# Two blocks of the first MLP moved into the last attention pair, weight bits through PSUM

## The chip, the core and the metric

The kernel runs on one core of a Trainium2 chip. The metric is device time in microseconds (us) of one execution, lower is better. The engines are PE (TensorE, matrix multiply, with its weight loads as PEld), DVE (VectorE), ACT (ScalarE), POOL (GpSimd) and SP (SyncE, which only issues transfers here). SBUF is the working memory; PSUM is the memory that matmuls write, eight banks of 128 x 512 f32.

## What is computed

Attention over 2 x 8 heads with 1152 keys and 576 pooled queries of width 64 (two neighbouring queries are averaged), then two MLPs over the 1152 resulting tokens, 512 wide inside and 2048 wide in between:

```python
q_pool = q.reshape(B, H, S // 2, 2, D).mean(axis=3)
scores = scale * np.matmul(q_pool, k.transpose(0, 1, 3, 2))
attn = softmax(scores)                      # row maximum subtracted
x = np.matmul(attn, v)                      # tokens: 2 x 576, features: 8 heads x 64
h = x @ w_in;  x = (max(h, 0) + alpha * min(h, 0)) @ w_out
h = x @ w_in2; x = (P(h) / (Q(h) + 1e-6)) @ w_out2
```

## The kernel before, in words

Precision is kept by splitting operands into a high and a low part, so most products are three matmuls. The weights come from memory as 64-bit patterns, and each block of them (128 x 512) is turned into f32 by hand: `w_load` (a transfer issued by SP into a raw slot), `w_abs` (ACT, takes the upper words into a work tile M), `w_shift` and `w_top` (DVE, change M in place, `w_top` with the raw upper words as second input), `w_low` (DVE, ors in the raw lower words), `w_hi` (ACT, high part), `w_lo` (POOL, low part). M is a slot of a small ring in SBUF, `ms`. A table `bits` can instead send the first three steps of a block through a PSUM bank, with `w_low` writing back into an SBUF slot; before, only blocks of the second MLP are in that table.

Everything is placed on one hand-written time axis. A function `at(time, fn, ...)` puts a step at a time in units of one attention step; `NUDGE` shifts single entries; `emit` sorts all entries by time and issues them. So the axis only sets the order on each engine's queue (and in SP's queue of transfers); what really happens when is settled by waits.

Attention runs over 8 pairs of heads (`p` = 0 to 7), 18 steps each: head `o` of the pair, key block `t` of 9. A step is `score` (PE, four matmuls into one of two PSUM buffers `st` of two banks each), `p_exp` (ACT, frees `st`), `p_lo` (DVE for the steps in `TAIL_DVE` or `ON_DVE`, POOL for the others) and, `LAG` = 3.348 steps later, `av` (PE, 15 small matmuls into the bank `o`; two neighbouring steps are put together). After a head, `norm` (DVE) empties bank `o`, and there is only one such bank. After a pair, `x_trans` (PE) turns the result into two banks, `x_hi` (ACT) and `x_lo` (DVE) write it into `xh` and `xl`, the first MLP's input. Inside a pair the row maxima for the next pair are made in the banks `m0`, `m1`, `m2` (`max_mm`, `max_relu`, `max_1`, `max_2`); in the last pair (times 126 to 144) there is no next pair, and these banks hold only the transposed result of pair 6, placed at 141.8.

The first MLP begins at time 144. `mlp_in(u)` is a block of 12 matmuls for step `u` = (layer, third of the tokens, block of the hidden width) into a bank `h0` to `h3`, which take the place of the two `st` buffers. The first four steps are of the first 384 tokens, which come from pairs 0 to 3 alone; from step 4 on the tokens need the last pair. Then come `act` and `prelu` (ACT, DVE), `g_hi` and `g_lo` (ACT, POOL) and `mlp_out` (PE, nine matmuls). The lists `wq` and `w_at` place the weights; the first nine blocks are prepared during pairs 6 and 7.

Of the kernel before, what the change touches and what calls it, by code (L numbers as in the profile page):

```python
# [11 lines left out]
F32 = mybir.dt.float32  # L12
# [9 lines left out]
P = 128  # L22

NUDGE = {
    "act 149.66": -1.83248,
    "act 149.84": 0.05243,
    "act 153.14": 0.05243,
# [5 lines left out]
    "av +15.34": -0.25933,  # L33
# [4 lines left out]
    "av +6.35": 0.11407,  # L38
    "av 118.34": -0.05915,
    "av 121.34": -0.27727,  # L40
    "av 121.35": 0.03902,
    "av 125.34": 0.28986,
    "av 125.35": 0.30551,
# [21 lines left out]
    "g_hi 1": -0.14597,  # L65
    "g_hi 151.56": -0.67127,
    "g_hi 154.86": -0.27922,
# [7 lines left out]
    "g_lo 148.36": 0.18778,  # L75
    "g_lo 154.96": -0.03704,
    "g_lo 244.06": 0.90746,
# [4 lines left out]
    "g_lo 352.74": 0.10763,  # L82
    "init_1 -59.90": -0.34567,
# [9 lines left out]
    "k2_move 108.36": 0.32169,  # L93
# [8 lines left out]
    "last 472.04": 5.6109,  # L102
    "load_k +13.00": 2.48384,
# [13 lines left out]
    "max_1 -51.55": 0.33187,  # L117
    "max_1 113.13": 0.14749,
    "max_1 120.30": -0.07283,
# [7 lines left out]
    "max_2 112.05": 0.42508,  # L127
    "max_2 117.78": 0.15996,
    "max_2 119.21": -0.07283,
# [8 lines left out]
    "max_mm 110.29": -0.29231,  # L138
    "max_mm 112.58": 0.05397,
    "max_mm 114.59": -0.08673,  # L140
    "max_mm 115.44": -0.77992,
    "max_mm 117.46": 0.28459,
    "max_mm 118.89": -0.21705,
    "max_mm 119.74": -0.07283,
    "max_mm 12.24": 0.03862,
    "max_mm 120.32": -0.07283,
    "max_mm 13.39": -0.15071,
    "max_mm 4.88": -0.12388,
    "max_put 13.64": -0.4836,
    "max_put 6.77": -0.05341,  # L150
    "max_relu -50.82": -0.13659,
    "max_relu 108.56": 0.29424,
    "max_relu 11.38": 0.04928,
    "max_relu 112.86": 0.20726,
    "max_relu 120.03": 0.0732,
# [17 lines left out]
    "mlp_consts 128.00": 0.28684,  # L173
    "mlp_in 2": -1.20185,
# [26 lines left out]
    "norm 146.76": 0.03824,  # L201
# [7 lines left out]
    "p_exp +16.45": -0.15163,  # L209
# [4 lines left out]
    "p_exp 121.45": -0.2674,  # L214
    "p_exp 122.45": -0.0253,
    "p_exp 143.45": 0.12204,
# [4 lines left out]
    "p_lo +12.05": 0.04903,  # L221
    "p_lo +2.05": 0.08012,
    "p_lo +5.05": 0.56187,
    "p_lo 1.05": 0.23379,
    "p_lo 11.05": 0.61317,
    "p_lo 113.05": 0.21679,
    "p_lo 122.05": -0.2674,
    "p_lo 123.05": 0.04433,
    "p_lo 124.05": 0.04433,
    "p_lo 128.05": -0.03096,  # L230
    "p_lo 129.05": 0.35293,
    "p_lo 135.05": -0.11243,
    "p_lo 17.05": 0.76834,
    "p_lo 5.05": -0.42349,
    "prelu 1": 0.06312,
    "prelu 160.51": -0.19632,
# [44 lines left out]
    "v_abs 112.00": 0.5906,  # L281
# [22 lines left out]
    "w_hi 125.13": 0.02594,  # L304
# [16 lines left out]
    "w_load 156.72": 0.44095,  # L321
# [35 lines left out]
def attention_then_two_mlps(  # L357
# [14 lines left out]
    nc = tc.nc  # L372
# [19 lines left out]
    psum = ctx.enter_context(tc.tile_pool(name="psum", bufs=1, space=bass.MemoryType.PSUM))  # L392
# [31 lines left out]
    xh = const.tile([P, KT, NTOK], F32R, name="xh")  # L424
    xl = const.tile([P, KT, NTOK], F32R, name="xl")
# [42 lines left out]
    bits = {}  # L468
# [71 lines left out]
    steps = [(0, T, f) for T in range(2) for f in range(NE)] + \  # L540
# [81 lines left out]
    KR, QR, QS, QH, QL, KH, KL, VR, VS, AM, X, NM, O, ST, TS = ({} for _ in range(15))  # L622
# [363 lines left out]
    for p in range(NP):  # L986
        b = S2 * p
        if p >= 2:
            k = S2 * (p - 2) + (-5.0 if p > 2 else 1.5)
            at(k, load_q, p)  # L990
            at(k, load_k, p)
            prep_at(S2 * (p - 2) + (5.2 if p > 2 else 9.6), p)
        if p >= 1:
            if p > 1:
                at(b - 23.0, load_v, p)
            m0, md = (b - 11.505, 1.15) if p == 1 else (b - 17.721, 1.433)
            for j in range(NJ2):
# [55 lines left out]
    for i in range(4):  # L1053
        at(k + (0.2, 1.285, 4.529, 5.1)[i], mlp_in, steps[i])
# [128 lines left out]
    for s, u in enumerate(steps):  # L1183
        L, T, f = u
# [90 lines left out]
```

## Time and profile before

| | before |
|---|---|
| time, median of 3 runs | 659.12 us (658.53 to 660.01) |
| the profiled execution | span 657.9 us from first to last instruction |
| busy share of the span | PE 96%, PEld 87%, DVE 76%, ACT 74%, POOL 63% |
| granted PE clock, mean over the span | 0.986 of full |

The profile is of one execution; the time of a run also holds what lies around the span. On this kernel the last attention pair lies at about 210 to 248 us of the span. Busy shares are means over stages with different limits.

### The profile page before, as it was taken

What the parts mean: (1) busy time and instruction counts of PE and PEld (TensorE: products, weight loads), DVE (VectorE), ACT (ScalarE), POOL (GpSimd) and SP (SyncE); (2) the same over time, 40 slices, a digit from 0 to 9 for tenths busy, and PEclk for the clock granted to TensorE, in tenths of its full rate; (3) what the DMA queues carried; (4) which work ended last, traced back from release to release, by engine and by line L of the source; (5) the groups of instructions that cost most, each with busy time, mean ns of one, the idle gap of its engine ahead of it and who ended that gap; (6) DMA issues with size and microseconds to landing.
All of it is one profiled execution on the core that took longest, in us unless ns stands there. A gap on an engine that the chain in (4) does not pass through costs nothing. (4 is left out here: it accounts for less than half of the span.)

```text
span 657.9 us, 13614 instructions
## 1 busy us (share of the span) xinstructions
PE 632.2 (96%) x5186; PEld 573.7 (87%) x5186; DVE 501.7 (76%) x941; ACT 485.6 (74%) x902; POOL 412.8 (63%) x350
## 2 busy tenths in 40 slices
PE   7789999999999789999999999999999999999997
PEld 6679999999998689999999999999898889999995
DVE  7877786876969988998851169996889777777764
ACT  6668778787887566677653478888888888778774
POOL 6557687787857775786762227785466745444443
PEclk7989999999999899999999999999999999999999
DMA  4887968869751225443420006641320010001001
GB/s 179 219 206 172 226 146 215 177 161 235 148 160 66 99 79 179 146 143 128 161 97 0 1 33 222 223 134 62 128 81 16 1 48 1 1 0 49 1 0 48
DMA packets 20960, 72.28 MB, mean 110 GB/s; under 512 B 3104, under 2 KB 3104, under 8 KB 20896
## 3 DMA queue, kind: packets, MB, share of 16 engines
q1 hardware_dynamic: 20896, 71.42, 37.6%
q8 instruction: 40, 0.66, 0.4%
q14 instruction: 24, 0.20, 0.1%
HBM read 47.72 MB, written 2.36 MB: 76 GB/s over the span
## 5 line engine op out<-in xcount | busy, mean ns | idle before, releaser
L874 POOL TENSOR_TENSOR PL<-PF 128x576 f16<-128x576 f32 x106 | 140.6, 1343 | 55.3 <-ACT PF L868 52.2
L1128 POOL TENSOR_TENSOR gl<-g,gh 128x384 fp32r<-128x384 f32 x96 | 106.4, 1108 | 74.5 <-ACT gh L1124 56.1
L868 ACT ACTIVATE PF<-st 128x576 f32<-128x576 f32 x144 | 91.7, 650 | 36.1 <-PE st L860 34.9
L1139 PE MATMUL acc<-woh,gl 128*128 128x512 f32 x288 | 113.8, 395 | 0.8 <-POOL gl L1128 0.8
L1139 PE MATMUL acc<-woh,gh 128*128 128x512 f32 x288 | 113.1, 393 | 0.7 <-ACT m L1170 0.7
L1139 PE MATMUL acc<-wol,gh 128*128 128x512 f32 x288 | 113.1, 393 | 0.0
L860 PE MATMUL st<-QQ,K 128*128 128x288 f32 (+1 forms) x576 | 103.9, 307 | 1.3 <-ACT PF L868 1.3
L1098 POOL TENSOR_TENSOR b<-a,b 128x384 f32<-128x384 f32 x48 | 49.0, 1020 | 78.1 <-ACT b L1086 78.1
L860 PEld LDWEIGHTS st<-QQ,K 128*128 128x128 f32 (+1 forms) x576 | 88.1, 193 | 2.7 <-ACT PF L868 1.7
L529 PE MATMUL hp<-xh,wih 128*128 128x384 f32 x384 | 83.4, 339 | 0.0
L529 PE MATMUL hp<-xl,wih 128*128 128x384 f32 x384 | 83.1, 338 | 0.0
L529 PE MATMUL hp<-xh,wil 128*128 128x384 f32 x384 | 83.0, 338 | 0.0
L886 PE MATMUL o<-V,PF 128*128 128x65 f16 x720 | 78.2, 196 | 2.9 <-DVE x L901 2.9
L773 PE MATMUL m<-K,QQ 128*128 128x384 f32 x234 | 72.0, 375 | 8.3 <-issue 2.5
L890 PE MATMUL o<-V,PL 128*128 128x65 f16 x720 | 76.6, 193 | 2.3 <-POOL PL L874 1.8
L886 PEld LDWEIGHTS <-PF 128*128 128x128 bf16 x720 | 67.0, 98 | 12.2 <-DVE x L901 3.3
L888 PE MATMUL o<-V,PF 128*128 128x64 f16 x720 | 77.3, 197 | 0.0
L529 PEld LDWEIGHTS hp<-xh,wih 128*128 128x128 f32 x384 | 69.6, 188 | 7.6
L890 PEld LDWEIGHTS <-PL 128*128 128x128 f16 x720 | 67.9, 100 | 2.7 <-POOL PL L874 2.0
L1124 ACT ACTIVATE gh<-g 128x384 fp32r<-128x384 f32 x96 | 50.0, 521 | 26.1 <-DVE g L1089 17.5
L529 PEld LDWEIGHTS hp<-xh,wil 128*128 128x128 f32 x384 | 68.7, 188 | 0.0
L529 PEld LDWEIGHTS hp<-xl,wih 128*128 128x128 f32 x384 | 68.6, 188 | 0.0
(143 smaller groups left out, 1360.5 us busy)
## 6 DMA issues: line engine op xcount, KB each, us to landing
K<-kh SPq DMA_DIRECT2D x28, 384.0 KB, 5.6
ring<-in_w SPq DMA_DIRECT2D x19, 512.0 KB, 3.6
raw<-in_w SPq DMA_DIRECT2D x13, 512.0 KB, 3.5
ring<-in_w1o SPq DMA_DIRECT2D x10, 512.0 KB, 3.4
qr<-in_qT SPq DMA_DIRECT2D x8, 576.0 KB, 7.6
vr<-in_v SPq DMA_DIRECT2D x8, 576.0 KB, 7.6
ring<-in_w2o SPq DMA_DIRECT2D x9, 512.0 KB, 4.3
QQ<-qh SPq DMA_DIRECT2D x14, 288.0 KB, 3.9
```

The costliest lines, as they stand in the source:

```text
L529: nc.tensor.matmul(hp, lhsT=w_[:, c * P:(c + 1) * P], rhs=x_[:, c, ts], start=k == 0, stop=k == 3 * KT - 1)
L773: nc.tensor.matmul(s[:, 0:CW], lhsT=of(QQ, n)[:, 0, k * P:(k + 1) * P], rhs=of(K1, n)[:, k0:k0 + CW], start=n == parts[0][0], stop=n == pa ...
L860: nc.tensor.matmul(st[:, hf, 0:HALF], lhsT=k_[:, ks], rhs=q_[:, c:c + HALF], start=first, stop=not first)
L868: nc.scalar.activation(out=PF[buf(n, t)][:, 0:SQ].rearrange("p (h q) -> p h q", h=2), in_=ST.pop((n, t))[:, :, 0:HALF], func=AF.Exp, scale=SC)
L874: e.tensor_tensor(out=PL[u][:, 0:SQ], in0=PF[u][:, 0:SQ], in1=top(PF[u])[:, 0:SQ], op=ALU.subtract)
L886: nc.tensor.matmul(o, lhsT=ph, rhs=V16[i][:, t, 0:D + 1], start=first, stop=False, skip_group_check=True)
L888: nc.tensor.matmul(o[:, 1:D + 1], lhsT=ph, rhs=V16[i][:, t, D + 1:2 * D + 1], start=False, stop=False, skip_group_check=True)
L890: nc.tensor.matmul(o, lhsT=pl, rhs=V16[i][:, t, 0:D + 1], start=False, stop=last, skip_group_check=True)
L1098: nc.gpsimd.tensor_tensor(out=E[u, "b"], in0=E[u, "a"], in1=E[u, "b"], op=ALU.mult)
L1124: nc.scalar.activation(out=G[u][0], in_=E[u, "g"], func=AF.Copy)
L1128: nc.gpsimd.tensor_tensor(out=gl, in0=E[u, "g"], in1=gh.bitcast(F32), op=ALU.subtract)
L1139: nc.tensor.matmul(acc, lhsT=g_[:, cs], rhs=w_, start=f == 0 and k == 0, stop=f == NF - 1 and k == 2)
```

## The change

Four things are changed. (1) Of the nine weight blocks that are prepared in pairs 6 and 7, the last six (`i >= 3`) send their bits through the bank `m0`. (2) `mlp_in` of the first two MLP steps (`EARLY = 2`) is cut into three parts of four matmuls, placed at 131.5, 133.5, 135.5 and 137.5, 139.5, 141.5 inside the last pair, into the banks `m1` and `m2`. (3) The transposes of pair 6 go from 141.8 to 130.2; those of pair 7 use `h0` and `h1` instead of `m1` and `m2`. (4) Some 200 entries of `NUDGE`, nearly all at times 108 to 161, are new or other. No instruction is added or taken out.

```diff
 NUDGE = {
...
+    "mlp_in 131.50": -0.04134,
+    "mlp_in 135.50": -0.97833,
+    "mlp_in 139.50": 0.50456,
+    "mlp_in 141.50": 0.73288,
+    "mlp_in 148.53": 0.41771,
...
-    "norm 146.76": 0.03824,
+    "norm 128.76": -0.05062,
+    "norm 146.76": 0.13528,
...
+    "p_lo 144.05": 0.08084,
...
+    "w_low 142.74": 1.10529,
...
+    EARLY = 2
...
     def hp_tag(u):
         s = steps.index(u)
+        if s < EARLY:
+            return f"m{s + 1}"
         return f"h{s % (2 if 4 <= s < PASS_B + 4 else 3 if PASS_B <= s < PASS_B + NF else 4)}"
 
-    def mlp_in(u):
+    def mlp_in(u, parts=(0, 1, 2)):
         L, T, f = u
         ts = slice(T * TOK, (T + 1) * TOK)
-        hp = HP[u] = bank(hp_tag(u), "hp")[:, 0:TOK]
+        if 0 in parts:
+            HP[u] = bank(hp_tag(u), "hp")[:, 0:TOK]
         wh, wl = W[L, f, "i"]
-        k = 0
-        for w_, x_ in ((wh, xh), (wh, xl), (wl, xh)):
+        for i in parts:
+            w_, x_ = ((wh, xh), (wh, xl), (wl, xh))[i]
             for c in range(KT):
-                nc.tensor.matmul(hp, lhsT=w_[:, c * P:(c + 1) * P], rhs=x_[:, c, ts],
-                                 start=k == 0, stop=k == 3 * KT - 1)
-                k += 1
+                nc.tensor.matmul(HP[u], lhsT=w_[:, c * P:(c + 1) * P], rhs=x_[:, c, ts],
+                                 start=i == c == 0, stop=i == 2 and c == KT - 1)
...
-            tp = X[p, c] = psum.tile([P, 512], F32, tag=f"m{c}", name="xtp")
+            tp = X[p, c] = bank(f"m{c}" if p + 1 < NP else f"h{c - 1}", "xtp")
...
-        x_at(b + S2 + 15.786 if p + 1 < NP else b + S2 + 5.0, p)
+        x_at(b + S2 + (15.786 if p + 2 < NP else 4.2 if p + 1 < NP else 5.0), p)
...
     for i, w in enumerate(wq[:NW]):
+        if i >= 3:
+            bits[w] = "m0"
         w_at(k + 0.475 + 3.778 * i, (4.178, 4.635, 5.665, 6.817, 8.104, 8.937), *w)
     k = S2 * NP
     at(k + 0.1, hp_rooms)
-    for i in range(4):
+    for i in range(EARLY):
+        for j in range(3):
+            at(k - 12.5 + 6 * i + 2 * j, mlp_in, steps[i], (j,))
+    for i in range(EARLY, 4):
         at(k + (0.2, 1.285, 4.529, 5.1)[i], mlp_in, steps[i])
```

## Rows read from the trace of the kernel before

**Rows 1.** Windows: us, busy by engine (instructions), granted clock, transfers.
```profile
210.00:220.00 10.00, 8.12 (x134) 7.31 (x130) 9.93 (x11) 6.81 (x13) 8.76 (x7) 1.00 0.18 56
220.00:230.00 10.00, 7.46 (x112) 7.24 (x113) 9.89 (x15) 5.95 (x11) 6.36 (x6) 0.83 0.29 107
230.00:240.00 10.00, 7.93 (x135) 7.07 (x134) 7.78 (x13) 6.06 (x11) 7.50 (x5) 1.00 0.20 68
...
260.00:280.00 20.00, 20.00 (x103) 18.26 (x102) 19.72 (x21) 12.48 (x25) 14.82 (x12) 1.00 0.38 139
```

**Rows 2.** Waits of PE, 200 to 246 us: us in total, times, longest.
```profile
PE o L886 <- DVE x L901: 2.9, 1, 2.9
PE o L890 <- POOL PL L874: 1.8, 2, 1.3
```

**Rows 3.** Timeline of DVE, 216 to 220 us: start, us, instruction.
```profile
216.09 0.78 DVE L478 TENSOR_SCALAR ring<-ring 128x512 int32<-128x512 int32 x1
216.91 1.52 DVE L483 SCALAR_TENSOR_TENSOR ring<-ring 128x512 int32<-128x512 int32 x1
218.46 1.52 DVE L491 SCALAR_TENSOR_TENSOR ring<-ring 128x512 int32<-128x512 int32 x1
```

**Rows 4.** Windows around PE's longest wait, columns as in Rows 1.
```profile
220.00:222.00 2.00, 0.00 (x0) 0.00 (x0) 1.93 (x4) 1.99 (x4) 2.00 (x2) 1.00 0.44 154
223.00:227.00 4.00, 4.00 (x57) 3.85 (x54) 3.96 (x6) 2.14 (x4) 1.06 (x2) 0.57 0.04 8
```

**Rows 5.** Line of POOL, 222 to 236 us: count, ns minimum/median/maximum, first and last start.
```profile
L874 POOL TENSOR_TENSOR PL<-PF x4: 1143/1462/4167, 222.7 to 235.7; 128x576 f16<-128x576 f32 x4
```

**Rows 6.** Groups of DVE, 208 to 245 us: count, busy us, mean ns, idle before.
```profile
L491 DVE SCALAR_TENSOR_TENSOR ring<-ring 128x512 int32<-128x512 int32 x4 | 4.5, 1126 | 0.0
L483 DVE SCALAR_TENSOR_TENSOR ring<-ring 128x512 int32<-128x512 int32 x4 | 4.2, 1053 | 0.0
L483 DVE SCALAR_TENSOR_TENSOR m<-ring,m 128x512 int32<-128x512 int32 x2 | 3.3, 1642 | 0.0
L478 DVE TENSOR_SCALAR ring<-ring 128x512 int32<-128x512 int32 x4 | 2.5, 632 | 0.0
...
L491 DVE SCALAR_TENSOR_TENSOR m<-ring,m 128x512 int32<-128x512 int32 x2 | 1.6, 789 | 0.0
...
L478 DVE TENSOR_SCALAR m<-m 128x512 int32<-128x512 int32 x2 | 1.0, 514 | 0.0
```

**Rows 7.** Lines of DVE, 400 to 560 us, columns as in Rows 5.
```profile
L483 DVE SCALAR_TENSOR_TENSOR bits<-ring,bits x14: 685/695/697, 402.1 to 512.4; 128x512 int32<-128x512 int32 x14
...
L478 DVE TENSOR_SCALAR bits<-bits x26: 687/692/700, 401.4 to 511.3; 128x512 int32<-128x512 int32 x26
...
L491 DVE SCALAR_TENSOR_TENSOR ring<-ring,bits x10: 677/686/689, 405.1 to 513.5; 128x512 int32<-128x512 int32 x10
```

**Rows 8.** Single line of DVE, 208 to 245 us, columns as in Rows 5.
```profile
L478 DVE TENSOR_SCALAR ring<-ring x4: 411/600/916, 208.3 to 232.0; 128x512 int32<-128x512 int32 x4
```

**Rows 9.** Timeline of PE, 238 to 268 us.
```profile
238.84 0.74 PE L917 MATMUL xtp<-ident,x 128*128 128x128 f32 x5
239.77 1.33 PE L860 MATMUL st<-QQ,K 128*128 128x288 f32 x8 [0.19 <-ACT PF L868]
...
242.00 0.97 PE L529 MATMUL hp<-xh,wih 128*128 128x384 f32 x4
...
246.33 0.20 PE L886 MATMUL o<-V,PF 128*128 128x65 f16 x1
...
267.11 0.39 PE L1139 MATMUL acc<-woh,gh 128*128 128x512 f32 x1
```

**Rows 10.** Timeline of DVE, 243 to 246 us.
```profile
243.17 0.81 DVE L925 TENSOR_TENSOR xl<-xtp,xh 128x512 fp32r<-128x512 f32 x2
...
244.72 0.75 DVE L874 TENSOR_TENSOR PL<-PF 128x576 f16<-128x576 f32 x1
```

**Rows 11.** Timeline of POOL, 264 to 266 us.
```profile
264.47 1.47 POOL L1128 TENSOR_TENSOR gl<-g,gh 128x384 fp32r<-128x384 f32 x1
```

More of the change, by code (lines that the diff above doesn't have):

```diff
@@ L24 @@
 NUDGE = {
-    "act 149.66": -1.83248,
+    "act 146.36": -1.10603,
+    "act 149.66": -1.72223,
     "act 149.84": 0.05243,
-    "act 153.14": 0.05243,
+    "act 152.96": 0.28197,
+    "act 153.14": 0.14335,
+    "act 156.26": -5.29814,
+    "act 156.44": -1.39004,
     "act 255.26": -0.04173,
@@ L32 @@
     "av +11.35": -0.00272,
-    "av +15.34": -0.25933,
+    "av +15.34": -0.05229,
+    "av +15.35": 0.10315,
     "av +17.35": 0.2086,
@@ L38 @@
     "av +6.35": 0.11407,
+    "av 109.34": 0.1927,
+    "av 109.35": 0.35589,
+    "av 114.35": 0.04355,
+    "av 116.34": -0.30193,
     "av 118.34": -0.05915,
[L40 to L43, printed above, removed]
+    "av 118.35": 0.48044,
+    "av 119.35": -0.29911,
+    "av 121.34": -0.94225,
+    "av 121.35": 0.06912,
+    "av 123.35": 0.12304,
+    "av 125.34": -0.02717,
+    "av 125.35": 0.44388,
+    "av 127.34": -0.28253,
     "av 130.34": 0.12379,
     "av 130.35": 0.38061,
+    "av 134.34": -0.21855,
+    "av 134.35": -0.05604,
+    "av 136.34": -0.02503,
+    "av 139.34": -0.50419,
+    "av 141.34": -0.0173,
     "av 143.34": -0.13888,
+    "av 143.35": 0.37695,
+    "av 145.34": -0.02526,
+    "av 145.35": 0.26536,
+    "av 146.35": 0.05461,
     "av 4.34": -0.09646,
@@ L65 @@
     "g_hi 1": -0.14597,
+    "g_hi 148.26": -0.05578,
     "g_hi 151.56": -0.67127,
-    "g_hi 154.86": -0.27922,
+    "g_hi 154.86": -0.34847,
+    "g_hi 158.16": -0.0454,
     "g_hi 2": 0.09897,
@@ L74 @@
     "g_hi 461.30": 0.10728,
-    "g_lo 148.36": 0.18778,
+    "g_lo 151.66": 0.29516,
     "g_lo 154.96": -0.03704,
+    "g_lo 158.26": 0.84439,
     "g_lo 244.06": 0.90746,
@@ L82 @@
     "g_lo 352.74": 0.10763,
+    "hp_rooms 144.10": 0.09744,
     "init_1 -59.90": -0.34567,
@@ L92 @@
     "k2_move +11.50": 4.60114,
-    "k2_move 108.36": 0.32169,
+    "k2_move 108.36": -0.36613,
     "k_diff +6.50": 0.25928,
@@ L102 @@
     "last 472.04": 5.6109,
+    "last_pair_rooms 126.50": 0.80603,
     "load_k +13.00": 2.48384,
@@ L117 @@
     "max_1 -51.55": 0.33187,
+    "max_1 108.83": -0.23804,
+    "max_1 111.70": 0.06062,
     "max_1 113.13": 0.14749,
-    "max_1 120.30": -0.07283,
+    "max_1 114.56": -0.03607,
+    "max_1 116.00": -0.13946,
+    "max_1 118.86": 0.04418,
     "max_1 15.10": -0.21038,
@@ L126 @@
     "max_2 -52.20": -0.12622,
-    "max_2 112.05": 0.42508,
+    "max_2 109.18": -0.22946,
+    "max_2 110.61": 0.04636,
+    "max_2 112.05": 0.95768,
+    "max_2 113.48": 0.3681,
     "max_2 117.78": 0.15996,
-    "max_2 119.21": -0.07283,
+    "max_2 119.21": 0.18431,
+    "max_2 120.64": -0.0839,
     "max_2 13.14": -0.24061,
@@ L137 @@
     "max_mm 0.58": -0.05411,
[L138 to L143, printed above, removed]
+    "max_mm 108.28": 0.25225,
+    "max_mm 108.86": 0.05718,
+    "max_mm 110.29": -0.24239,
+    "max_mm 112.58": 0.1727,
+    "max_mm 113.16": -0.27666,
+    "max_mm 114.01": -0.07202,
+    "max_mm 114.59": -0.13974,
+    "max_mm 116.88": -0.45352,
+    "max_mm 117.46": 0.15243,
+    "max_mm 118.89": -0.15077,
     "max_mm 119.74": -0.07283,
     "max_mm 12.24": 0.03862,
-    "max_mm 120.32": -0.07283,
+    "max_mm 120.32": -0.49667,
     "max_mm 13.39": -0.15071,
     "max_mm 4.88": -0.12388,
+    "max_put 122.58": 0.27584,
     "max_put 13.64": -0.4836,
@@ L151 @@
     "max_relu -50.82": -0.13659,
-    "max_relu 108.56": 0.29424,
     "max_relu 11.38": 0.04928,
-    "max_relu 112.86": 0.20726,
-    "max_relu 120.03": 0.0732,
+    "max_relu 110.00": -0.23787,
+    "max_relu 112.86": 0.24883,
+    "max_relu 120.03": -0.10014,
     "max_relu 7.93": 0.56196,
     "max_rows +14.31": -0.08493,
+    "max_rows 122.31": 0.05726,
     "max_rows 13.37": -0.4561,
@@ L160 @@
     "max_split 12.24": 0.27587,
+    "max_split 121.18": -0.04134,
     "max_split 16.84": 0.72017,
@@ L173 @@
     "mlp_consts 128.00": 0.28684,
+    "mlp_consts 133.00": 0.16871,
+    "mlp_in 131.50": -0.04134,
[3 more added lines that the diff above has]
+    "mlp_in 148.53": 0.41771,
+    "mlp_in 158.20": -0.0609,
     "mlp_in 2": -1.20185,
@@ L182 @@
     "mlp_out 1": -2.76993,
+    "mlp_out 153.25": 0.1283,
+    "mlp_out 156.55": 0.04691,
     "mlp_out 3": -0.14864,
@@ L186 @@
     "mlp_out 466.75": 0.51976,
+    "mlp_rooms 150.50": -0.42802,
     "newton 307.86": 0.15744,
@@ L208 @@
     "p_exp +10.45": -0.06749,
-    "p_exp +16.45": -0.15163,
+    "p_exp +15.45": 0.18536,
+    "p_exp +16.45": -0.11413,
+    "p_exp +17.45": -0.06943,
     "p_exp +6.45": -0.11489,
@@ L213 @@
     "p_exp 117.45": 0.3022,
-    "p_exp 121.45": -0.2674,
+    "p_exp 119.45": 0.02991,
+    "p_exp 120.45": -0.11183,
+    "p_exp 121.45": -0.36953,
     "p_exp 122.45": -0.0253,
-    "p_exp 143.45": 0.12204,
+    "p_exp 124.45": 0.30542,
+    "p_exp 125.45": -0.05638,
+    "p_exp 126.45": -0.38716,
+    "p_exp 127.45": -0.47427,
+    "p_exp 128.45": 0.26012,
+    "p_exp 130.45": 0.03501,
+    "p_exp 132.45": -0.16805,
+    "p_exp 136.45": -0.09432,
+    "p_exp 140.45": -0.07307,
+    "p_exp 141.45": -0.07144,
+    "p_exp 142.45": 0.09075,
+    "p_exp 143.45": 0.24749,
     "p_exp 3.45": 0.46905,
@@ L221 @@
     "p_lo +12.05": 0.04903,
+    "p_lo +16.05": 0.15039,
+    "p_lo +17.05": 0.10815,
     "p_lo +2.05": 0.08012,
@@ L224 @@
     "p_lo 1.05": 0.23379,
+    "p_lo 108.05": 1.71774,
+    "p_lo 109.05": 0.96994,
     "p_lo 11.05": 0.61317,
-    "p_lo 113.05": 0.21679,
-    "p_lo 122.05": -0.2674,
-    "p_lo 123.05": 0.04433,
+    "p_lo 110.05": -0.26813,
+    "p_lo 111.05": 1.75388,
+    "p_lo 112.05": -0.91528,
+    "p_lo 113.05": -0.47992,
+    "p_lo 114.05": 1.43444,
+    "p_lo 116.05": 0.0379,
+    "p_lo 118.05": 0.46394,
+    "p_lo 119.05": -0.24861,
+    "p_lo 120.05": 0.30854,
+    "p_lo 121.05": -0.06126,
+    "p_lo 123.05": 0.18759,
     "p_lo 124.05": 0.04433,
-    "p_lo 128.05": -0.03096,
+    "p_lo 125.05": 0.4012,
+    "p_lo 127.05": 0.13444,
+    "p_lo 128.05": 0.23929,
     "p_lo 129.05": 0.35293,
+    "p_lo 130.05": 1.0792,
+    "p_lo 132.05": 0.51744,
+    "p_lo 133.05": 0.35944,
     "p_lo 135.05": -0.11243,
+    "p_lo 137.05": -0.14399,
+    "p_lo 138.05": 0.49851,
+    "p_lo 139.05": 2.20425,
+    "p_lo 141.05": 0.9817,
+    "p_lo 142.05": -0.22956,
+    "p_lo 144.05": 0.08084,
     "p_lo 17.05": 0.76834,
@@ L235 @@
     "prelu 1": 0.06312,
-    "prelu 160.51": -0.19632,
+    "prelu 150.61": -0.66085,
+    "prelu 153.91": -0.32945,
+    "prelu 157.21": 0.76971,
+    "prelu 160.51": -0.48479,
     "prelu 252.91": -0.76034,
@@ L267 @@
     "score 0.00": 0.035,
+    "score 108.00": -0.04102,
     "score 110.00": 0.1155,
+    "score 111.00": -0.41693,
     "score 112.00": -0.46662,
-    "score 113.00": -0.60286,
-    "score 118.00": 0.37261,
-    "score 120.00": 0.1067,
+    "score 113.00": -0.73168,
+    "score 116.00": -2.6424,
+    "score 119.00": -0.18599,
+    "score 120.00": -1.45253,
     "score 121.00": -0.41706,
     "score 122.00": -0.93559,
+    "score 123.00": 0.13775,
+    "score 124.00": 0.27913,
     "score 125.00": -0.7719,
-    "score 135.00": -0.55352,
-    "score 141.00": 0.06003,
+    "score 127.00": -2.66496,
+    "score 128.00": 0.02083,
+    "score 129.00": -0.06616,
+    "score 132.00": -0.07978,
+    "score 134.00": -0.0657,
+    "score 135.00": -0.55352,
+    "score 136.00": -0.293,
+    "score 137.00": -0.58351,
+    "score 138.00": 0.00442,
+    "score 139.00": -0.29725,
+    "score 142.00": 0.20166,
     "score 8.00": -0.42927,
@@ L280 @@
     "v_abs -49.53": 2.0347,
-    "v_abs 112.00": 0.5906,
+    "v_abs 112.00": 0.63011,
     "v_hi +14.96": -2.44725,
@@ L284 @@
     "v_hi 1.97": -0.0338,
-    "v_hi 122.96": -0.05458,
+    "v_hi 113.19": 0.20356,
+    "v_hi 131.19": 0.20924,
     "v_hi 14.96": 0.46325,
+    "v_lo +15.69": -1.30354,
     "v_lo +5.92": 0.08909,
-    "v_lo 123.69": -0.0255,
+    "v_lo 113.92": 0.17612,
+    "v_lo 131.92": -0.28225,
     "v_max +5.40": 0.37337,
     "v_max -47.98": 1.78699,
+    "v_max 113.40": 0.2898,
     "v_max 9.38": 0.15233,
@@ L295 @@
     "w_abs 1": 0.08196,
+    "w_abs 121.21": -0.29279,
+    "w_abs 124.99": -0.35527,
+    "w_abs 128.76": 0.12472,
     "w_abs 132.54": -0.19784,
-    "w_abs 153.93": 0.30825,
+    "w_abs 136.32": 0.2053,
+    "w_abs 140.10": 0.44434,
+    "w_abs 153.93": 0.37728,
     "w_abs 157.06": 0.44095,
-    "w_abs 160.20": 0.47734,
+    "w_abs 160.20": 0.41807,
     "w_abs 2": -0.46434,
@@ L303 @@
     "w_hi 0": 0.24713,
-    "w_hi 125.13": 0.02594,
+    "w_hi 132.69": -0.06541,
+    "w_hi 136.47": 0.16651,
+    "w_hi 140.25": -0.02612,
+    "w_hi 144.02": 0.12937,
+    "w_hi 147.80": 0.25057,
     "w_hi 154.45": 0.15249,
@@ L310 @@
     "w_lo 0": 0.256,
-    "w_lo 118.41": -0.47373,
-    "w_lo 133.52": 0.51392,
+    "w_lo 118.41": -0.60898,
+    "w_lo 133.52": 0.20586,
+    "w_lo 137.30": -0.02673,
+    "w_lo 141.08": 4.02398,
     "w_lo 144.86": -0.31586,
-    "w_lo 148.64": 0.21196,
-    "w_lo 154.55": 2.59363,
+    "w_lo 148.64": 2.50932,
+    "w_lo 154.55": 2.39976,
     "w_lo 157.69": 0.44095,
+    "w_lo 160.82": 1.41328,
     "w_lo 2": 3.88308,
@@ L320 @@
     "w_load 117.03": 0.09064,
-    "w_load 156.72": 0.44095,
+    "w_load 120.81": -0.38484,
+    "w_load 128.37": -0.05019,
+    "w_load 135.92": 0.26143,
+    "w_load 147.31": -1.89704,
+    "w_load 150.44": -3.78195,
+    "w_load 153.58": 0.47245,
+    "w_load 156.72": 0.61107,
     "w_load 159.85": 0.44095,
@@ L324 @@
     "w_load 296.83": -0.17914,
-    "w_low 116.29": 0.08664,
+    "w_low 116.29": 0.18019,
+    "w_low 120.07": -0.0845,
     "w_low 123.85": -0.53747,
-    "w_low 135.18": -0.07142,
-    "w_low 146.52": -0.14543,
+    "w_low 135.18": -0.68451,
+    "w_low 138.96": -0.20937,
+    "w_low 142.74": 1.10529,
+    "w_low 146.52": -0.08582,
+    "w_low 153.17": -0.57349,
+    "w_low 156.30": 0.20595,
+    "w_low 159.44": 0.25883,
     "w_low 352.60": 0.14453,
@@ L331 @@
     "w_shift 121.67": -0.2674,
-    "w_shift 125.44": 0.73028,
+    "w_shift 125.44": 0.83144,
+    "w_shift 136.78": 0.08967,
+    "w_shift 140.56": 0.0275,
     "w_shift 151.44": -0.25643,
+    "w_shift 154.58": -0.02618,
+    "w_shift 157.71": 0.20611,
+    "w_shift 160.85": 0.24925,
     "w_shift 300.53": 0.17955,
@@ L336 @@
     "w_top 0": 0.51732,
-    "w_top 115.14": 0.76013,
+    "w_top 115.14": 0.02872,
     "w_top 118.92": -0.77142,
-    "w_top 130.25": -0.2934,
+    "w_top 130.25": 0.26819,
+    "w_top 134.03": -0.40551,
     "w_top 141.59": 0.95071,
-    "w_top 152.53": 0.36648,
     "w_top 155.67": 0.44095,
@@ L346 @@
     "warm -58.62": 1.87459,
-    "x_hi +16.29": -0.36444,
-    "x_hi 124.29": -0.41997,
-    "x_hi 142.29": -0.2355,
+    "x_hi +16.29": 0.24347,
+    "x_hi 124.29": 0.06389,
     "x_hi 149.50": 0.35742,
+    "x_lo +16.69": 0.91515,
     "x_trans +15.79": -0.03344,
-    "x_trans 123.79": -0.36729,
+    "x_trans 123.79": -0.32324,
 }
```

## The prediction

> **What bounds the kernel now.** I read the page's busy shares first, then windows of ten us, then the waits of PE, then single timelines where PE stood still. PE is busy for 96% of the span, so time can be won only where PE is idle or slow. In the first MLP it is neither: 260:280 is full, at full clock [rows 1]. It is idle inside the last pair: 1.88 us in 210:220, 2.54 in 220:230 and 2.07 in 230:240, together 6.5 us, and in the same windows DVE is busy for 9.93, 9.89 and 7.78 of 10 [rows 1]. So the last pair is paced by DVE, not by PE.
>
> The waits say how. The longest is 2.9 us: the first `av` of the pair's first head waits for `norm` of the head before, which frees the one bank `o` [rows 2]. DVE had no idle time ahead of that `norm`; it was late, with `w_shift`, `w_top` and `w_low` of one weight block (0.78, 1.52, 1.52 us) close in front of it [rows 3]. That wait costs a second time: PE does nothing from 220 to 222 us, and in 223:227 the granted clock is 0.57 on average, that is mostly the lower of its two levels (1.2 instead of 2.4 GHz) [rows 4]. Over 4 us that loses 4 x 0.43 = 1.7 us. The next wait, 1.3 us, is for a `p_lo` on POOL [rows 2]; the longest of these instructions took 4.17 us where the shortest took 1.14 [rows 5].
>
> **Weight bits through PSUM.** In 208:245 DVE did the three bit steps of six blocks out of SBUF: 4.2 + 3.3 us of L483, 4.5 + 1.6 of L491, 2.5 + 1.0 of L478, together 17.1 us or 2.85 per block [rows 6]. The second MLP shows the same steps with the bits in PSUM: 0.695, 0.692 and 0.686 us in the median, 2.07 per block, and within 0.02 us of that every time [rows 7]. Six blocks change over, so DVE gets 6 x 0.78 = 4.7 us shorter. `w_shift` alone gets longer (0.69 against 0.58 on average); the two steps with two inputs get shorter, since out of SBUF their means lie between 0.79 and 1.64 us [rows 6].
>
> POOL is busy for 6.4 to 8.8 of 10 us where they are slow [rows 1]. The Trainium skill, SBUF — State Buffer, section Who interferes with whom, states it as a rule: a VectorE instruction with two SBUF inputs contends with a GpSimd instruction that reads SBUF, one with at most one such input does not. By that rule the trace agrees: bits in PSUM leave one SBUF input, and the spread is gone. The Trainium skill, VectorE: DVE Perf Modes, section Why PSUM operands drop a tier, speaks against the change: a PSUM operand holds f32 work at the plain rate. The trace agrees: the fastest `w_shift` out of SBUF took 0.41 us [rows 8], out of PSUM all took 0.69. By that page alone, with nothing won on the other two, six blocks would make DVE 6 x 0.28 = 1.7 us longer; by the rows it is 4.7 us shorter, and the rows decide.
>
> What is this worth on PE? The fourth block is the one in front of the late `norm`: 3.82 us there [rows 3] become 2.07, so `norm` comes 1.75 us earlier and the wait of 2.9 shrinks to 1.15. Bounds: nothing (if DVE is then held elsewhere) to 2.9. I take 1.75. The 2.07 us of idle time in 230:240 left the clock at 1.00 [rows 1], so I take it that the 1.7 us of slow clock go too; if not, they stay in the sum.
>
> `m0` is one bank for six blocks, where a ring gave slack: `w_abs` of the next block waits on ACT until `w_low` of the last is done, with `p_exp` queued behind it. By the times given these two stand 0.04 steps apart once (143.84 and 143.88) and 0.9 steps or more otherwise; the price is at most one `w_low`, 0.69 us [rows 7], once. I take 0.
>
> **Two blocks moved.** In the old order the 24 matmuls run from 242.00 to 246.33 us, 4.33 us [rows 9]. They leave that place: -4.33. They cost the same in the last pair, +4.33, less what they fill of idle PE time. Behind the first piece lie the 2.07 us of idle time in 230:240 [rows 1]. Bounds of the fill: 0 to 2.07, plus whatever new slack the pieces find. I take 2.07: the idle time is in pieces of up to 1.3 us, and a piece is 4.33/6 = 0.72 us, so it fits in without holding the scores long. The blocks need weights finished long before and tokens of pairs 0 to 3, so nothing else can hold them but their banks.
>
> **What the move uncovers.** In the old order these blocks also hid the end of the pair: the last scores end at 239.77 + 1.33 = 241.10, the last `p_lo` on DVE at 244.72 + 0.75 = 245.47 [rows 9, 10], 4.4 us later, and PE spent 4.33 of them on the two blocks. Now only `av` work stands there. One pair of steps of it fills 241.10 to 242.00, 0.9 us [rows 9]; two such pairs stand between the last score and the last `av`, 1.8 us. If DVE is as late as before, PE idles 4.4 - 1.8 = 2.6 us; if DVE is free, it doesn't. DVE is 4.7 us lighter by then and xl of pair 6 (0.81 us [rows 10]) no longer stands there. I take 0.7.
>
> **Transposes of pair 6.** Work is the same. But the first piece needs the bank `m1`, so it waits on PE until `x_lo` of pair 6 has read it, with all later scores behind it. In the old place the chain from transposes to the end of xl took 238.84 to 243.98, 5.1 us [rows 9, 10], of which the transposes and xl themselves are 1.55; the rest is ACT's part and queueing. PE has 0.74 us of transposes, 0.9 of `av` and half of 1.33 of scores [rows 9] in between: 2.3 us. So the stall is 0 to 2.8. In the new place only two 0.69 us steps [rows 7] are placed between `norm` and xl on DVE, so I take 0.4. The transposes of pair 7 use free banks of the same kind: 0.
>
> **The rest of the order.** The other shifts (pair 6, first MLP steps) move instructions of equal cost. I count nothing; the 1.88 us of idle time in 210:220 [rows 1] bound a gain, and a loss could be as large. The front of the MLP must follow: in 260:280 DVE is busy for 19.72 of 20 [rows 1], and PE uses a `gl` at 267.11 that is ready at 264.47 + 1.47 = 265.94 [rows 9, 11], 1.2 us of slack. PE can get more than 1.2 us ahead only if DVE does too; its 4.7 us allow that.
>
> **Sum.** -4.33 + 4.33 - 2.07 - 1.75 - 1.7 + 0.7 + 0.4 = -4.4 us. The profiled span is 657.9; the median of the runs is 659.12, 1.2 more, which I leave as it is. Span 653.5, time 654.7 us.
>
> **Rivals.** (a) A new wait takes the place of the old one: the chain of pair 6 stays at 5.1 us, the first piece stands 2.8 us at the head of PE's queue, and as after the old wait the clock falls, 1.7. With scores held that long the fill of 2.07 is lost. -1.75 - 1.7 + 0.7 + 2.8 + 1.7 = +1.8, 660.9 us, slower. It decides from a chain of some 4.6 us on. For it: DVE is full there. Against: the bit steps in front of xl are among those that get shorter. Chance 0.08.
>
> (b) The contention only moves: POOL then meets the ten `p_lo` on DVE that still read SBUF twice, `norm` is as late as before, and the clock falls. -2.07 + 0.7 + 0.4 = -1.0, 658.1, no difference to be measured. The MLP front gives the same limit, 1.2. Chance 0.1.
>
> (c) The tail stays open: 2.6 instead of 0.7, so -2.5, 656.6 us. Chance 0.15.
>
> (d) All waits of PE in the pair go, since POOL too is freed: 6.5 + 1.7 - 0.7 - 0.4 = 7.1, 652.0 us. By the Trainium skill's rule on contention (SBUF — State Buffer, section Who interferes with whom), only the weight steps stop contending, not the `p_lo` on DVE, which speaks for a part of it. Chance 0.12.
>
> The forecast, between the others, has 0.55. About 0.2%, 1.3 us, is what a measurement here can tell from no change. Faster: 0.55 + 0.15 + 0.12 = 0.82; same 0.1; slower 0.08. The range reaches from (d) to (b) and its bounds: 651.8 to 658.4.
>
> **What would show it.** L483 and L491 on bits at 0.69 us in the last pair. PE's wait for `norm` near 1.2 us and the clock at 1.00 throughout 220:230. Pieces of `mlp_in` between scores, with less than 4.5 us of idle PE from 210 us to the end of the scores. After the last score an idle PE of under 1 us. If instead the longest wait is that of a piece for xl, (a) holds; if it is still for `norm`, (b). The prediction is wrong at its root if the pair gets longer by the whole 4.3 us, that is if PE was not truly free there.

## The result

The changed kernel took 652.78 us in the median of 5 runs (651.85 to 656.65), the old one beside it 660.01 (658.53 to 661.81): a ratio of 0.990 with a 95% interval of 0.9873 to 0.9926, so 4.9 to 8.4 us faster. 4.4 us were forecast. The profiled spans are 650.8 and 657.9 us.

Not all of these 7.1 us of span come from the last pair: the first twelve heads, hardly touched by the change, took from 189.4 to 195.3 us in the traces of this study. A cleaner measure is the rest of the span behind the `norm` of head 11 (heads counted from 0; it starts at 190.56 us in the old trace and 189.81 in the new). It is 467.34 us before and 460.99 after, 6.35 us less. All comparisons of traces below use it, and call it the rest.

Windows of the new kernel, columns as in [rows 1]:

```profile
210.00:220.00 10.00, 8.00 (x124) 7.18 (x122) 9.86 (x15) 7.81 (x15) 8.89 (x7) 1.00 0.34 106
220.00:230.00 10.00, 10.00 (x163) 9.76 (x161) 9.87 (x17) 6.94 (x14) 5.09 (x6) 1.00 0.17 57
230.00:240.00 10.00, 10.00 (x179) 9.71 (x178) 8.33 (x14) 7.08 (x13) 5.62 (x5) 1.00 0.39 121
240.00:250.00 10.00, 9.87 (x65) 8.80 (x62) 8.61 (x16) 7.61 (x17) 6.30 (x6) 1.00 0.57 207
...
260.00:280.00 20.00, 20.00 (x103) 18.05 (x102) 19.76 (x22) 13.40 (x26) 16.12 (x12) 1.00 0.41 144
```

PE has no idle time left from 220 to 240 us, where it had 4.6 [rows 1], and the granted clock is at its upper level throughout. What is left is 2.0 us in 210:220. The waits of PE from 200 to 246 us:

```profile
PE st L1003 <- ACT PF L1011: 0.9, 1, 0.9
PE xtp L1060 <- DVE x L1044: 0.9, 1, 0.9
PE o L1029 <- DVE x L1044: 0.4, 1, 0.4
PE o L1033 <- POOL PL L1017: 0.2, 1, 0.2
```

The wait of 2.9 us for `norm` [rows 2] is gone. (The second line is the transposes' wait for a `norm`; the transposes of pair 6 now stand ahead of the `av` that waited before. The third line is of another `norm`, at 205 us.) The timeline of DVE ahead of that `norm`, to be laid beside [rows 3]:

```profile
215.24 0.68 DVE L619 TENSOR_SCALAR bits<-bits 128x512 int32<-128x512 int32 x1
215.96 0.70 DVE L624 SCALAR_TENSOR_TENSOR bits<-ring,bits 128x512 int32<-128x512 int32 x1
216.69 0.69 DVE L632 SCALAR_TENSOR_TENSOR m<-ring,bits 128x512 int32<-128x512 int32 x1
217.29 1.26 DVE L1017 TENSOR_TENSOR PL<-PF 128x576 f16<-128x576 f32 x1
218.48 0.15 DVE L1042 TENSOR_SCALAR sm<-o 128x5 f32<-128x5 f32 x1
```

3.82 us of bit steps became 2.07, and `norm` (the last line) starts 3.05 us earlier than before, 2.3 of it won behind the `norm` of head 11. All six blocks run at that rate (lines by tile, 205 to 250 us: count, ns minimum/median/maximum):

```profile
L619 DVE TENSOR_SCALAR bits<-bits x6: 684/692/700, 215.2 to 239.6; 128x512 int32<-128x512 int32 x6
L624 DVE SCALAR_TENSOR_TENSOR bits<-ring,bits x6: 680/693/697, 216.0 to 240.3; 128x512 int32<-128x512 int32 x6
L632 DVE SCALAR_TENSOR_TENSOR ring<-ring,bits x4: 673/681/689, 222.4 to 241.1; 128x512 int32<-128x512 int32 x4
L632 DVE SCALAR_TENSOR_TENSOR m<-ring,bits x2: 679/683/687, 216.7 to 232.9; 128x512 int32<-128x512 int32 x2
```

GpSimd gains as well. Its `p_lo` took up to 4.17 us [rows 5]; now, from 218 to 245 us, the longest takes 1.66:

```profile
L1017 POOL TENSOR_TENSOR PL<-PF x7: 1143/1147/1659, 217.9 to 237.7; 128x576 f16<-128x576 f32 x7
```

And the pieces of the first two MLP blocks stand between the scores, each four matmuls (timeline of PE, 222 to 243 us; the last line is already the third block, behind the last scores). From the start of a piece to the start of the next instruction it is 0.71 to 0.79 us; the column shows more, since the next instruction starts before the piece has ended:

```profile
221.63 0.91 PE L673 MATMUL hp<-xh,wih 128*128 128x384 f32 x4
224.47 0.87 PE L673 MATMUL hp<-xl,wih 128*128 128x384 f32 x4
227.26 0.87 PE L673 MATMUL hp<-xh,wil 128*128 128x384 f32 x4
230.55 0.95 PE L673 MATMUL hp<-xh,wih 128*128 128x384 f32 x4
...
240.29 0.94 PE L673 MATMUL hp<-xh,wih 128*128 128x384 f32 x4
```

### The profile page after: what moved, and what is told of

It reads as the page before. It is cut to its first block, busy times and chain, and to the rows that moved or that the text cites. A ratio compares the mean times of both kernels' runs of the same rounds, so it can differ in the third digit from the quotient of the medians.

```text
span 650.8 us, 13635 instructions
## 1 busy us (share of the span) xinstructions
PE 630.1 (97%) x5186; PEld 571.3 (88%) x5186; DVE 496.2 (76%) x941; ACT 485.8 (75%) x902; POOL 408.0 (63%) x350
## 5 line engine op out<-in xcount | busy, mean ns | idle before, releaser
L1017 POOL TENSOR_TENSOR PL<-PF 128x576 f16<-128x576 f32 x106 | 136.8, 1304 | 56.3 <-ACT PF L1011 52.8
L1029 PE MATMUL o<-V,PF 128*128 128x65 f16 x720 | 76.7, 194 | 0.4 <-DVE x L1044 0.4
L1031 PE MATMUL o<-V,PF 128*128 128x64 f16 x720 | 75.9, 196 | 0.0
```

Source lines behind the costliest of these rows:

```text
L1017: e.tensor_tensor(out=PL[u][:, 0:SQ], in0=PF[u][:, 0:SQ], in1=top(PF[u])[:, 0:SQ], op=ALU.subtract)
L1029: nc.tensor.matmul(o, lhsT=ph, rhs=V16[i][:, t, 0:D + 1], start=first, stop=False, skip_group_check=True)
L1031: nc.tensor.matmul(o[:, 1:D + 1], lhsT=ph, rhs=V16[i][:, t, D + 1:2 * D + 1], start=False, stop=False, skip_group_check=True)
```

## Experiments: which part makes the gain

The theory is that of the prediction: VectorE paced the last pair through bit steps that met GpSimd at SBUF; bits in PSUM take that away, and the blocks then fill idle PE time. The rivals: the moved blocks do it alone, the new order does it, or the ring slots that the bits set free do it. Under each run stands what was expected of it.

Here the change has three parts: the bits, the move (the blocks with the transposes) and the new order, which is the table `NUDGE`. That makes eight combinations, the old and the new kernel among them. Here are the other six.

**Bits alone** (`e1_bits`), in the old kernel:

```diff
     for i, w in enumerate(wq[:NW]):
+        if i >= 3:
+            bits[w] = "m0"
```

> The old kernel with one change alone: the last six weight blocks send their bits through the bank m0. Theory (VectorE paced the last pair because its two-input bit steps out of SBUF met GpSimd): the norm in front of PE's longest wait comes about 1.75 us earlier, the wait falls from 2.9 to about 1.2, the clock stays at full, and the kernel is 2 to 4 us faster. Rival (the moved blocks alone make the gain): within 1 us of the old kernel.

**The move with the new order, without the bits** (`e2_move`): the new kernel without these two lines.

> The new kernel without the bits in PSUM (they stay in the SBUF ring), all else as in the new kernel. Theory: the pieces only fill the idle time behind the long wait, so about 2 us faster than the old kernel, with a wait for norm of over 2 us and bit steps of up to 1.5 us and more. Rival (the moved blocks alone): 5 to 7 us faster, like the new kernel.

**Bits and move with the old order** (`e3_oldorder`): the new kernel with the old `NUDGE`.

> The new kernel with the old table of shifts. Theory (the structure makes the gain, the shifts only polish it): 4 to 6 us faster than the old kernel. Rival (the new order is what makes it): under 2 us faster, or slower.

**The new order alone** (`e4_neworder`): the old kernel with the new `NUDGE`.

> The old kernel with the new table of shifts; entries of steps that it lacks do nothing. Theory (structure): within 1.5 us of the old kernel, to either side. Rival (order): 2 us faster or more.

**The move alone** (`e7_move_old`): the new kernel without the bits and with the old `NUDGE`.

> The moved blocks without the bits in PSUM and with the old table of shifts: the corner that is missing. Theory as the first four runs leave it (without lighter VectorE work the pair stays as long, the pieces only lengthen it and the end loses its cover): within 2 us of the old kernel, PE idle by 2 us or more behind the last scores. Rival (it was the new order that spoilt the move when run without the bits): 2 us faster or more.

**Bits with the new order, no move** (`e8_bits_new`): the new kernel with the blocks and the transposes in their old places and banks.

> The bits in PSUM with the new table of shifts, but no moved blocks. Theory (the new order is made for the moved blocks): about as fast as the bits with the old order, 2.5 to 4 us faster than the old kernel. Rival (the new order wins 1 us by itself once VectorE is lighter): 4 to 5 us faster.

| bits | move | new order | kernel | ratio to the old kernel (95%) | rest of the span, us against old |
|---|---|---|---|---|---|
| | | | old | 1 | 0 |
| | | x | e4_neworder | 1.0011 (0.9992 to 1.0031) | +0.55 |
| | x | | e7_move_old | 0.9992 (0.9980 to 1.0004) | -0.13 |
| | x | x | e2_move | 1.0022 (1.0003 to 1.0041) | +0.89 |
| x | | | e1_bits | 0.9956 (0.9936 to 0.9976) | -3.41 |
| x | | x | e8_bits_new | 0.9971 (0.9955 to 0.9987) | -3.23 |
| x | x | | e3_oldorder | 0.9914 (0.9887 to 0.9940) | -5.13 |
| x | x | x | new | 0.9900 (0.9873 to 0.9926) | -6.35 |

The last column is one execution each, the ratio is the timing; they agree within a us but for `e8_bits_new` (0.9971 is 1.9 us, the trace says 3.2). Kernels that gain nothing lie between -0.18 and +0.89 in that column (two of them follow below), so one us there is not told from chance. Three things follow. The bits are the root: with them every combination is faster, without them none measurably is. The move is worth nothing without them; with them it is worth 1.7 to 3.1 us by the traces (-5.13 against -3.41, -6.35 against -3.23) and 2.8 to 4.7 by the timings, and in the new order the two intervals lie well apart. The new order is worth 1.2 us by the traces where both other parts are there and costs 0.2 to 1.0 elsewhere; this is not shown, since it is no more than the scatter and the intervals of the last two lines overlap.

`e1_bits` came out by the theory in its details too: `norm` came 2.18 us earlier behind that of head 11, 0.9 us of PE's wait for it were left, and the clock was at full. `e3_oldorder`, `e4_neworder` and `e7_move_old` lie where the theory put them; `e8_bits_new` does by the trace, while its timing is under the 2.5 us.

The expectation of 2 us for `e2_move` failed, and with it a step of the prediction (the fill, below). The pieces did fill idle time, but the idle time came back behind them. In the move alone, PE in 244:247 us, then its waits from 238 to 252 us, then DVE there:

```profile
244.00:247.00 3.00, 1.73 (x32) 1.61 (x33) 2.97 (x4) 1.63 (x3) 1.71 (x2) 1.00 0.16 44
```

```profile
PE o L892 <- POOL PL L876: 0.9, 1, 0.9
PE xtp L919 <- DVE x L903: 0.9, 1, 0.9
PE o L892 <- DVE PL L876: 0.6, 1, 0.6
```

```profile
241.86 1.77 DVE L483 SCALAR_TENSOR_TENSOR m<-ring,m 128x512 int32<-128x512 int32 x1
243.66 1.52 DVE L491 SCALAR_TENSOR_TENSOR m<-ring,m 128x512 int32<-128x512 int32 x1
245.11 0.75 DVE L876 TENSOR_TENSOR PL<-PF 128x576 f16<-128x576 f32 x1
```

This is the end of the pair: the last `p_lo` waits on DVE behind two bit steps of 1.77 and 1.52 us, and the `av` on PE for it. In the old order the two blocks stood here as cover [rows 9, 10]. DVE is busy for 2.97 of the 3 us in which PE is for 1.73. So without a lighter DVE the blocks only change places with idle time.

**The place of the operand or the ring** (`e6_slack`): the new kernel with the six blocks' bits in one SBUF slot of their own.

```diff
+    extra.append(hold.tile([P, DM], F32, name="extra"))
...
-        M[L, f, nm] = bank(tag, "bits") if tag else take(ms)
+        M[L, f, nm] = extra[0] if tag == "sbuf" else bank(tag, "bits") if tag else take(ms)
...
-            bits[w] = "m0"
+            bits[w] = "sbuf"
```

> The new kernel, but the six blocks' bits go through one slot of SBUF of their own instead of the bank m0. The ring gets the same relief and the blocks the same single slot, but the two-input steps read SBUF twice. Theory (it is the place of the operand: two SBUF inputs meet GpSimd): slow bit steps of 1.4 us and more are back, the wait for norm is over 2 us, time within 2 us of the old kernel. Rival (the ring slots are what helps): 5 to 7 us faster, like the new kernel.

1.0013 (0.9996 to 1.0029), rest +0.05 us: nothing is left of the gain, though the ring has the same relief. The bit steps, 205 to 250 us:

```profile
L620 DVE TENSOR_SCALAR extra<-extra x6: 427/696/1219, 218.7 to 248.9; 128x512 int32<-128x512 int32 x6
L625 DVE SCALAR_TENSOR_TENSOR extra<-ring,extra x6: 691/1518/1775, 219.6 to 249.3; 128x512 int32<-128x512 int32 x6
L633 DVE SCALAR_TENSOR_TENSOR ring<-ring,extra x3: 679/682/691, 228.5 to 247.4; 128x512 int32<-128x512 int32 x3
L633 DVE SCALAR_TENSOR_TENSOR m<-ring,extra x2: 680/1100/1519, 221.1 to 241.7; 128x512 int32<-128x512 int32 x2
```

For `w_top` (the second line): same instruction, same shape, same place in the order, and 0.69 us in the median with one operand in PSUM, 1.52 with both in SBUF. It is the place of the operand.

Not every step with two SBUF inputs is slow, as the third line shows. What tells the slow ones from the others is GpSimd. In the old kernel (lines of POOL and DVE): from 216.54 to 220.99 us GpSimd is at work on `p_lo`, and both two-input bit steps that fall into it take 1.52 us [rows 3]; from 237.30 to 239.79 it has nothing to do, and `w_low`, one of the two, takes 0.68:

```profile
216.54 4.45 POOL L874 TENSOR_TENSOR PL<-PF 128x576 f16<-128x576 f32 x3
239.79 1.15 POOL L874 TENSOR_TENSOR PL<-PF 128x576 f16<-128x576 f32 x1 [2.50 <-ACT PF L868]
237.84 0.68 DVE L491 SCALAR_TENSOR_TENSOR ring<-ring 128x512 int32<-128x512 int32 x1
```

So it is in all fourteen traces of this study, from 196 to 250 us. The 41 two-input bit steps out of SBUF beside which no GpSimd instruction ran took 0.68 or 0.69 us each; the 130 that met one took 0.68 to 1.77; the 88 with an operand in PSUM took 0.67 to 0.70, GpSimd or not. The Trainium skill, SBUF — State Buffer, section Who interferes with whom, has the rule: a VectorE instruction with two SBUF inputs contends with a GpSimd instruction that reads SBUF, and one with a single SBUF input does so only in the modes that use two ports. The traces agree on the two-input steps. The prediction gave the rule without its second condition, and that is too short: `w_shift` out of SBUF, with one input, took 0.41 to 0.43 us beside an idle GpSimd (25 times) and up to 1.50 beside a busy one; out of PSUM it took 0.68 to 0.70. No run took GpSimd's work away, so its part is shown by the overlap in time alone.

## Experiments: the wait, the clock, and a further step

**The clock** (`e5_fill`): the prediction had PE lose 1.7 us to a slow clock behind the 2.9 us wait. 16 matmuls into the idle bank `m0` fill the wait:

```diff
+    def fill(n):
+        f = bank("m0", "fill")
+        for _ in range(n):
+            nc.tensor.matmul(f[:, 0:TOK], lhsT=xh[:, 0, 0:P], rhs=xh[:, 0, 0:TOK], start=True, stop=True)
+    at(130.33, fill, 16)
```

> The old kernel with 16 matmuls of 384 columns more, into the idle bank m0, placed in PE's queue right in front of the av that waits 2.9 us for norm; their result is read by nobody. They take about 2.8 us, so PE stands no longer but the norm comes no earlier. Theory (the wait costs a second time through the clock, 1.7 us): the clock stays at full in 220 to 230 us and the part of the span behind the eleventh norm gets 1 to 1.7 us shorter, time 0 to 2 us less. Rival (what follows the wait is paced by other engines, so the clock cost nothing): full clock, but no change of over 0.5 us.

1.0012 (0.9995 to 1.0029), rest -0.18 us. Single us of it:

```profile
224.00:225.00 1.00, 1.00 (x22) 0.91 (x20) 1.00 (x3) 0.87 (x2) 0.00 (x0) 1.00 0.00 0
...
229.00:230.00 1.00, 0.00 (x0) 0.00 (x0) 1.00 (x3) 0.63 (x2) 0.47 (x1) 1.00 0.00 0
...
233.00:234.00 1.00, 1.00 (x16) 0.85 (x16) 1.00 (x3) 0.91 (x2) 0.20 (x1) 0.50 0.00 0
```

The clock is full where it was 0.57 [rows 4], and PE, now ahead, stands idle at 229 us with DVE busy all the time; then the clock falls after all, to its lower level. The slow stretch moved by some nine us. So this run does not price the clock by itself; it shows that PE ahead by the wait and at full clock ran into the next wait, for DVE, and that the pair got no shorter.

**One block, or the other five** (`e9_one` with `i == 3`, `e10_rest` with `i > 3`, in the old kernel):

> The old kernel, with the bits of one block alone in PSUM: the fourth, whose steps stand in front of the late norm. It tells the two parts of the bits' 3.4 us apart. Theory (the first part is the shorter wait, and with it the clock stays at full): norm 2 us earlier, full clock in 220 to 230 us, and the span behind the eleventh norm 2 to 3.5 us shorter. Rival (what counts is VectorE's whole work in the pair; a PE that comes earlier waits later): norm 2 us earlier, but under 1.5 us left at the end.

> The old kernel, with the bits of the last five blocks in PSUM and the fourth in SBUF. Theory (wait and clock): the wait for norm of 2.9 us and the slow clock stay, 0 to 1 us shorter. Rival (VectorE's whole work): the wait stays, but 1.5 to 3 us of it are won back before the end.

`e9_one`: 0.9987 (0.9968 to 1.0006), rest -1.55 us. `norm` came 2.19 us earlier behind that of head 11, the clock stayed full from 205 to 250 us, and part of it was handed back. Its waits of PE and a window:

```profile
PE o L890 <- DVE PL L874: 2.9, 3, 1.3
PE st L860 <- ACT PF L868: 1.8, 3, 1.1
PE o L886 <- DVE x L901: 0.9, 1, 0.9
```

```profile
225.00:235.00 10.00, 6.80 (x112) 6.11 (x112) 9.96 (x15) 5.60 (x12) 5.26 (x6) 1.00 0.21 59
```

The wait for `norm` fell from 2.9 to 0.9, the waits for a `p_lo` on DVE rose to 2.9; PE is idle for 3.2 of 10 us with DVE at 9.96. `e10_rest`: 0.9957 (0.9940 to 0.9974), rest -1.13 us. The wait of 2.9 us is there as before, and so is the slow clock, for longer:

```profile
225.00:235.00 10.00, 9.62 (x133) 9.34 (x133) 7.90 (x15) 4.64 (x10) 4.54 (x5) 0.66 0.20 68
```

Yet it is faster. Here DVE has 2.1 us to spare and PE is busy, for most of the time at the lower level of its clock. So the two parts of the bits' gain are about equal by the traces (1.55 and 1.13 of 3.41); the timings lean to the second (0.9 and 2.8 us). The trace of `e10_rest` is of the longest of its 12 executions (661.48 us, median 657.56). Which part is larger stays open. By the timings both runs came out as their rival, VectorE's whole work, has it; by the traces they lie between it and the theory. `e9_one`, with the wait cut to 0.9 us and the clock at full, gave less than half of the 3.45 us that the prediction had put on the two.

**A further block** (`e11_five`, `e12_both`): what is left of PE's idle time lies ahead of `norm`. The third block's bits were sent through `m0` too, right behind the maxima; the second kernel also has `TAIL_DVE` begin with 2 instead of 1, so that one `p_lo` in front of `norm` goes to GpSimd.

```diff
-        if i >= 3:
+        if i >= 2:
...
-        w_at(k + 0.475 + 3.778 * i, (4.178, 4.635, 5.665, 6.817, 8.104, 8.937), *w)
+        w_at(k + 0.475 + 3.778 * i, (4.178, 4.635, 5.665, 6.817, 8.104, 8.937) if i != 2 else
+             (5.87, 6.17, 6.67, 7.37, 8.6, 9.4), *w)
```

> The new kernel, and the third block too sends its bits through m0, with its bit steps about one step later, when the maxima have left the bank. Theory (contended bit steps in front of norm hold PE): the norm comes 0.5 to 1.5 us earlier than in the new kernel, the time is 0 to 1.5 us under the new one's, 0.988 to 0.990 of the old. Rival (that wait is now set by the maxima and the values' split on VectorE): no change against the new kernel, 0.990.

> The kernel of the run before with one p_lo on VectorE exchanged: the second step of the pair goes to GpSimd and the third to VectorE, behind norm. Theory (whatever stands in front of norm on VectorE holds PE): norm 0.7 us or more earlier than in the run before, time 0 to 1 us less. Rival (GpSimd then gives that step late, and av waits for it): no change or up to 1 us more.

Both are worse than the new kernel: 0.9961 (0.9943 to 0.9979) and 0.9976 (0.9955 to 0.9997), rest -3.43 and -2.51. `e11_five` missed theory and rival; its `norm` came 2.35 us later than in the new kernel, behind that of head 11. In `e12_both` it came no earlier than in `e11_five` and the time was 0.7 us more, which is that run's rival. In `e11_five` the wait of ACT and that of PE:

```profile
ACT bits L614 <- DVE ring L632: 1.6, 1, 1.6
```

```profile
PE st L1003 <- ACT PF L1011: 3.0, 2, 2.6
```

`w_abs` of the fourth block stood on ACT until `w_low` of the third had left the one bank, two `p_exp` stood behind it, and PE waited 2.6 us for the score buffer. This is the price that the prediction had put at zero for the new kernel, and there it is zero: the new kernel's ACT has no such wait from 205 to 245 us. It did occur in `e1_bits`, 5.1 us in four waits, without a like wait of PE:

```profile
ACT bits L473 <- DVE ring L491: 3.9, 2, 2.3
...
ACT bits L473 <- DVE m L491: 1.2, 2, 1.1
```

Nothing tried here beats the new kernel.

## Why the prediction was right, and where its sizes were off

The direction, the main mechanism and the range held; the size was 4.4 us where 7.2 (by the timings) or 6.35 (by the rest of the span) came. Two terms of the sum, the clock and the fill, rested on reasons that the runs do not bear out.

- **Bits through PSUM**, 2.07 us a block: right, 2.07 measured, and shown by `e6_slack` to be the operand's place. The relief was a little less than said: the six blocks of [rows 6] hold the third, which does not change, and not the ninth, which does. The right six took 16.7 us before, so DVE got 4.3 us shorter and not 4.7. No term of the sum hangs on it.
- **The wait for `norm`**, -1.75 and a wait of 1.15 us left: right, `norm` came 2.3 us earlier in the new kernel and 2.19 in `e9_one`, where 0.9 us of wait were left. Of what is over 1.75, 0.44 us are the `p_lo` in front of `norm`, 1.26 us long where it had been 1.70.
- **The clock**, -1.7 on top: the clock did stay full, but as a term of its own this was wrong. `e9_one` had it full, and the earlier `norm` too, and gained 1.55 us by the trace and 0.9 by the timing, not 3.45; PE that comes earlier waits later as long as DVE sets the pace. (`e5_fill` can't tell, its slow stretch only came later.) In its place stands what the prediction left out: the other five blocks' lighter DVE, about as much (`e10_rest`, -1.13 by the trace, 2.8 by the timing). That the bits alone then gave 3.41 us where 3.45 had been added up is luck.
- **The fill**, -2.07 whatever DVE does (rival (b) keeps it with DVE as late as before): the step that failed in its reasoning. Without the bits the move gave -0.13 us and, in the new order, +0.3; with them -1.7 and -3.1. The term held because the bits were there.
- **The uncovered end**, +0.7, and **the bank of the first piece**, +0.4: both too dear. In the new kernel PE is idle for 0.13 us in 240:250, and it has no wait for xl at all. The end's upper bound of 2.6 us was no invention: the move alone has PE idle for 2.4 us from there on (0.22, 1.27 and 0.91 in three windows from 241 to 250 us).
- **The rest of the order**, 0: 1.2 us by the traces, once both other parts were there, but no more than the scatter; not shown to be other than 0.
- **The front of the MLP** had to follow, and did: 260:280 is full on PE.

With the two debits at 0.1 and 0 instead of 0.7 and 0.4, and the order at -1.2, the same sum would have come to -6.6, near what was measured; but it still holds the clock term that was wrong in kind, so that this too is in part luck. Of the rivals, (d), all waits gone and 652.0 us, came nearer to the measured 652.78 than the forecast of 654.7: 220 to 240 us is full, and 2.0 us are left in 210:220. It had been given a chance of 0.12 because ten `p_lo` on DVE still read SBUF twice; they still do, with 0.90 us on average against 0.99 before, but no wait of PE for one of them is left.

## What to carry to other kernels

Moving work into idle time of one engine pays only if the engine that makes it idle is also relieved; in this kernel the idle time else came out again where the moved work had stood as cover. Where two-input steps of VectorE are slow beside a busy GpSimd, try one operand in PSUM, even if a one-input step beside them gets slower for it (here 0.69 us against 0.58 on average). One bank for a row of blocks is a queue of its own: a producer that waits for it holds everything behind it on its engine, as ACT did in `e11_five`, so its order has to be set with that in mind.

## What the runs showed that was not expected

The contention cost GpSimd more than VectorE in single cases: one `p_lo` took 4.17 us where the shortest took 1.14 [rows 5], while the two bit steps of VectorE that ran beside it took 0.68 each; with the bits in PSUM the longest took 1.66. And a lower clock of PE need not undo a gain: `e10_rest` had a mean of 0.66 over ten us and was faster than the old kernel all the same.
